# Gated sliding-window attention and channel MLP: early q/k writes, statistics, y and DRAM copies at other steps, first weights in another layout, last output in halves

## The chip, the cores and the metric

The kernel runs on one core of one Trainium2 chip. The metric is the time of one execution on the device in microseconds. A core has five engines with instruction streams of their own: TensorE (PE in the profile, its weight loads are PEld), VectorE (DVE), ScalarE (ACT), GpSimd (POOL) and SyncE (SP), which here only issues DMAs. DMAs are issued by SP and, where named, by ACT; "SPq" and "ACTq" are these issues. Each engine works strictly in the order in which its instructions were written, and waits at an instruction until the semaphores that it needs have come.

## The reference

For x of 2048 tokens by 512 features, two branches are mixed by a gate of each token (cut to what matters):

```python
def _A_ref(x, wqkv, wo):              # H = 32 heads, Dh = 16, W = 256
    q, k, v = split(x @ wqkv)
    scores = einsum("bhqd,bhkd->bhqk", q, k) * (Dh ** -0.5)
    mask = (idx[:, None] - idx[None, :] >= 0) & (idx[:, None] - idx[None, :] < W)
    p = softmax(where(mask, scores, -1e9))
    return merge_heads(p @ v) @ wo
def _B_ref(x, w1, b1, w2, b2):        # F = 1792
    h = gelu(layernorm(x) @ w1 + b1)
    return h @ w2 + b2
g = sigmoid((x * gate_w).sum(-1, keepdims=True))
return g * _A_ref(x, wqkv, wo) + (1 - g) * _B_ref(x, w1, b1, w2, b2)
```

All is float32. To keep its precision, most products are made of three: each operand is split into a high part h in a shorter format and a low part l = x - h, and h*h + h*l + l*h is summed.

## The kernel before, in words

Sizes: tokens go in 4 chunks c of 512 and 16 blocks of 128; features in 4 tiles dt of 128; the heads in 4 groups g of 8, and a group in two halves, which makes 8 attention passes p of 4 heads each; the MLP's 1792 hidden features in 14 tiles f.

**First stage** (from `first_units`, line 242, to `settle`): q, k and v for all tokens, layer-norm statistics, and the normalised x (called y), transposed. Its work is a list of units n = 0 to 47 with three matmul groups of 4 each: `QK(g, t, c)` (line 281) makes q (t = 0) or k (t = 1) of one group and chunk, `vl[b]` (line 305) makes v of a block. Before each unit `tick()` (line 130) advances a step; `after(k, fn)` puts work off by k steps, and `at(n, fn)` (line 542) puts work ahead of unit n. So a step is one unit, and the order of every queue is written by these two.

- `first_units` is the first chunk's q and k, interleaved with the arrival of x and of the first weights. `load_x` loads x chunks on SP and splits them, `copy` (line 121) on ACT and `lo_part` (line 118) on DVE.
- `qk_out` (line 291) evicts q or k from PSUM: ACT copies the high part to a tile t, DVE makes the low part, and both go to DRAM (`qkd`): high, low and, for a second operand order, the high part again. For group 0 the high part is written twice by ACT; for other groups once by ACT, and `double` (line 300) copies it from DRAM to DRAM later. The low part is written by SP a step later.
- `load_stacks` (line 318) loads q and k columns from DRAM into the tile `qk`, the operands of the scores. `gaps` (line 200) fills constant rows.
- `stat_unit` (line 431) takes mean, variance and gate of a block on DVE. `stat_end` (line 444) makes the inverse root on POOL for half the tokens, and puts it into DRAM over a DVE transpose. `load_y` (line 474) loads it back and x with it; its `rest` subtracts and multiplies on POOL (lines 489, 490), and its `fin` splits on ACT and DVE. `load_w1` (line 505) loads and splits MLP weights.
- Every third step from 13 on has an `s_pair` (line 327): scores with tokens as rows, of which DVE takes the row maxima (lines 345, 346). `put_max` (line 350) sends four blocks of maxima over POOL, a DVE transpose and DRAM into extra rows of `qk`; in the second stage its four parts are put off by the numbers of `CHAIN` (line 52), counted in letters of `ORDER`.

All temporaries of this stage are tiles t from 15 buffers in turn (`t2`, line 82): a new one waits until the old one's last reader, a DMA too, is done. PSUM has 4 banks "d" for q, k and v, and 2 for S.

**Second stage** (`run(ORDER)`, line 722): attention passes p = 0 to 7, with the MLP's first product in between. The string `ORDER` gives the order: S is an `s_pair`, T an `st_pair` (line 382: transposed scores, exponential on ACT, masks on POOL), P a `pv` (line 402), f two matmuls of `mlp1_unit` (line 597). S runs ahead of T by ten blocks. At each block kb of a pass, `block` (line 684) issues the stacks for the next pass, and some of the copies of `double`.

**Third stage** (from line 759): gelu and the second MLP product (`mlp2`, line 813, 4 x 14 items), whose results are added to the attention output: `attn_out` (line 768) loads what `pv` stored, scales it and multiplies with wo (line 799). The last item of a chunk adds the sum from PSUM on DVE (line 825) and writes it out by SP (line 826).

A tile "edge" of 128 x 8 float32 values stands at the top end of SBUF, and the large tiles x8 below it.

## Time and profile before

| | us |
|---|---|
| median of 3 runs | 720.76 |
| lowest, highest | 718.58, 721.39 |
| the profiled execution | 721.59 |
| its span on the core | 719.9 |
| first stage, to the first transposed scores | 0 to 154.2 |
| second stage, to the last transposed scores | 154.2 to 504.2 |

The profile is of one execution. Times in it are microseconds from the start of the span unless marked ns. A timeline row has its start, its duration, engine, line, operation, output <- inputs, shapes, the count of merged instructions, and in brackets how long the engine was idle before it and what released it. A row of waits has engine, tile and line, the releaser, and us in total, times, longest. A row of stretches has the busy time and instructions of the five engines, then the granted clock of PE as a share, the mean busy share of the 16 DMA engines, and GB/s. A group's row ends with busy us and mean ns, then idle time before it. A row of the chain has start, duration and what the chain went through. A row of a line's instructions has the count, the durations in ns as lowest/median/highest, and the first and last start.

### The profile page before, as it was taken

How to read it: one execution, taken by the hardware profiler on the slowest of the kernel's cores; microseconds unless marked ns; L12 is line 12 of the kernel's file. 1: busy time of each engine (PE TensorE's matmuls, PEld its weight loads, DVE VectorE, ACT ScalarE, POOL GpSimd, SP SyncE). 2: the span in 40 equal slices, each digit the busy share in tenths (PEclk: the TensorE clock that was granted, in tenths of full speed). 3: DMA queues.
4: the chain of work that ended last, by engine and by line, in shares of the span. 5: the costliest groups of instructions: out<-in, count | busy, mean ns of one | idle time of the engine just before them, and what ended most of it. 6: DMA issues, size and time to landing. Idle time of an engine off the chain costs nothing.

```text
span 719.9 us, 15913 instructions
## 1 busy us (share of the span) xinstructions
PE 702.1 (98%) x5740; PEld 541.8 (75%) x5740; DVE 472.6 (66%) x977; ACT 366.5 (51%) x580; POOL 288.6 (40%) x647
## 2 busy tenths in 40 slices
PE   9899999989999899999999999999999999999997
PEld 6677777767777577777777777777777788888885
DVE  6327886777786577767777687784556745645544
ACT  5323123346778567667777767767533414123121
POOL 9220219975557456555665657558000000000000
PEclk9999999989999999999999999999999999999999
DMA  9999795864667765567746664624865443542531
GB/s 312 287 309 290 217 300 159 279 186 153 204 203 222 227 207 163 169 202 237 214 142 203 188 196 141 187 87 162 264 220 164 159 147 118 164 138 103 180 104 58
DMA packets 102917, 137.92 MB, mean 192 GB/s; under 512 B 13912, under 2 KB 54040, under 8 KB 102712
## 3 DMA queue, kind: packets, MB, share of 16 engines
q1 hardware_dynamic: 95544, 124.59, 55.4%
q10 hardware_dynamic: 7296, 12.32, 5.4%
q8 instruction: 46, 0.75, 0.5%
q14 instruction: 31, 0.25, 0.1%
HBM read 81.53 MB, written 54.30 MB: 189 GB/s over the span
## 4 chain that ended last, share of the span: by engine, by line
PE 68%; DMA 12%; POOL 7%; DVE 4%; SPq 3%; ACT 2%; issue 2%; ACTq 2%; POOLq 0%; DVEq 0%
PE ps_b L609 21%; PE ps_a L820 16%; PE ps_b L410 12%; PE ps_b L391 7%; PE ps_b L336 6%; PE ps_o L799 6%; DMA qk<-t 3%; POOL t L489 3%; POOL t L490 3%; DMA qk<-qk 2%; DMA t<-in_xa 2%; ACTq L297 1%; ACT t L122 1%; DMA t<-in_wqk 1%; DMA wv<-in_wqk 1%
## 5 line engine op out<-in xcount | busy, mean ns | idle before, releaser
L609 PE MATMUL ps_b<-x,w 64*128 64x512 f32 x1344 | 215.1, 399 | 0.7 <-DVE mx L346 0.4
L395 POOL TENSOR_SCALAR_AFFINE_SELECT p<-p 128x256 f32<-128x256 f32 x344 | 131.9, 412 | 97.7 <-ACT p L393 96.9
L393 ACT ACTIVATE p<-ps_b 128x768 f32<-128x768 f32 (+2 forms) x184 | 137.5, 770 | 42.6 <-PE ps_b L391 35.6
L820 PE MATMUL ps_a<-x,t 128*128 128x512 f32 x648 | 154.6, 395 | 0.1
L346 DVE TENSOR_REDUCE mx<-ps_b 128x2 f32<-128x512 f32 x208 | 144.1, 693 | 7.1
L820 PEld LDWEIGHTS ps_a<-x,t 128*128 128x128 f32 x648 | 121.4, 188 | 30.3 <-DVE t L119 0.8
L609 PEld LDWEIGHTS ps_b<-x,w 64*128 64x128 f32 x1344 | 131.7, 188 | 12.6 <-issue 2.8
L345 DVE COPY_PREDICATED ps_b<-tri,ps_b 128x256 f32<-128x256 uint8 x208 | 88.3, 425 | 53.4 <-PE ps_b L336 39.1
L336 PE MATMUL ps_b<-qk 62*128 62x384 f32 (+2 forms) x472 | 86.4, 349 | 6.3 <-DMA qk<-qk 4.0
L391 PE MATMUL ps_b<-qk 50*128 50x384 f32 (+5 forms) x512 | 91.1, 345 | 0.4 <-DVE mx L346 0.3
L287 PE MATMUL ps_d<-x,w 128*128 128x512 f32 x360 | 88.6, 397 | 0.0
L287 PEld LDWEIGHTS ps_d<-x,w 128*128 128x128 f32 x360 | 66.9, 188 | 17.2 <-issue 1.9
L410 PE MATMUL ps_b<-p,v 128*32 128x256 f32 (+1 forms) x1376 | 75.5, 332 | 0.7 <-ACT p L393 0.7
L122 ACT ACTIVATE t<-ps_b 128x512 f32<-128x512 f32 (+1 forms) x112 | 51.9, 490 | 42.2 <-PE ps_b L410 35.5
L395 POOL TENSOR_SCALAR_AFFINE_SELECT x<-x 128x256 f32<-128x256 f32 x136 | 52.4, 411 | 37.9 <-ACT x L393 37.4
L391 PEld LDWEIGHTS ps_b<-qk 50*128 50x128 f32 (+1 forms) x512 | 51.7, 186 | 20.0 <-issue 5.8
L393 ACT ACTIVATE x<-ps_b 128x768 f32<-128x768 f32 (+2 forms) x72 | 55.1, 778 | 18.0 <-PE ps_b L391 13.9
L336 PEld LDWEIGHTS ps_b<-qk 62*128 62x128 f32 (+1 forms) x472 | 47.3, 187 | 22.3 <-issue 7.3
L410 PEld LDWEIGHTS ps_b<-p,v 128*32 128x32 f32 x1376 | 39.1, 110 | 26.7 <-ACT p L393 3.7
L119 DVE TENSOR_TENSOR t<-t,t 128x512 fp32r<-128x512 f32 x70 | 48.5, 692 | 14.6 <-ACT t L122 11.6
L312 PE MATMUL ps_d<-wv,x 128*128 128x512 f32 x192 | 49.5, 406 | 2.9 <-DVE wv L119 2.6
L122 ACT ACTIVATE t<-t 128x512 fp32r<-128x512 f32 x16 | 10.1, 632 | 77.8 <-DVE t L787 39.4
(80 smaller groups left out, 661.7 us busy)
## 6 DMA issues: line engine op xcount, KB each, us to landing
qk<-qk SPq DMA_DIRECT2D x112, 196.0 KB
t<-hp SPq DMA_DIRECT2D x56, 256.0 KB
hp<-t SPq DMA_DIRECT2D x52, 256.0 KB
qk<-t ACTq DMA_DIRECT2D x40, 256.0 KB
qk<-t SPq DMA_DIRECT2D x32, 256.0 KB
osc<-t SPq DMA_DIRECT2D x31, 256.0 KB
t<-in_w SPq DMA_DIRECT2D x28, 256.0 KB
w<-w SPq DMA_DIRECT2D x28, 256.0 KB
```

The costliest lines, as they stand in the source:

```text
L122: act.activation(dst, src, AF.Copy)
L287: pe.matmul(o, a[:, dt * 128:(dt + 1) * 128], b[:, dt * C:(dt + 1) * C], start=n == 0, stop=n == 11)
L312: pe.matmul(o, x[:, a:a + 128], wvs[dt][:, k], start=n == 0, stop=n == 11)
L336: pe.matmul(o[:, e, :n], qs[pr][r:k, qb * 128:qb * 128 + 128], ks[pr][r:k, t0:t0 + n], start=True, stop=True)
L345: dve.copy_predicated(o[:, :, :128], tri, o[:, :, 256:384])
L346: dve.tensor_reduce(m, o[:, :, :256], mybir.AxisListType.X, ALU.max)
L391: pe.matmul(o[:, e, :w], ks[pr][r:k, kb * 128:kb * 128 + 128], qs[pr][r:k, kb * 128:kb * 128 + w], start=True, stop=True)
L393: act.activation(pt[:, :, :w], o[:, :, :w], AF.Exp, scale=0.25)
L395: pool.affine_select(out=pt[:, :, a:a + 128], in_=pt[:, :, a:a + 128], pattern=[[0, 2], [sgn, 128]], base=b, channel_multiplier=-sgn, comp ...
L410: pe.matmul(a[32 * h:32 * h + 32, at:at + w], vs[:, kb, v:v + 32], pts[p, kb][:, h, fr:fr + w], start=n == 0, stop=n == len(parts) - 1, sk ...
L609: pe.matmul(o[:, e], w[kt // 4][r:r + 64, k, m:m + 128], y[r:r + 64, a:a + C], start=n == 0, stop=n == 23)
L820: pe.matmul(accs[c][b], x[:, b * 128:(b + 1) * 128], w, start=f == 0 and n == 0, stop=f == FT - 1 and n == 2)
```

## The change

Nine edits, all of order, place or shape; what is computed stays the same.

- `qk_out`: for group 0 all three writes are issued by SP, two steps later for chunk 0 and one step later for the others; for other groups the high part stays on ACT.
- `load_stacks` of pass 0 at steps 7, 8, 9, 12 in place of 4, 6, 8, 12; the low parts of the v weights at step 4 in place of 5.
- The first weights come in an array of their own, `wq0`, with both t side by side, in pieces of dt 0, dt 1 and dt 2 to 3; `first_units` splits them by dt, and the first x copy goes to DVE.
- Statistics: `stat_end` at 21 and 29 (22 and 30), its write after 2 steps (3); `load_y` at 25 and 33 (26 and 35), with lag 2 (3), and `fin` at lag + 2 (lag + 3); first w1 loads at 38 and 41 (41 and 44).
- `double` copies one t at a time, at every even block of passes 0, 2 and 4; before, both at every odd block from 9 on of passes 0, 1 and 3.
- `CHAIN`'s last number is 30 (28).
- `attn_out(0)` at f = 3 (4), its matmuls after 2 steps (1).
- The last block's last output is computed in halves of 256 columns, and the second half written by ACT.
- "edge" has 104 values per partition (8), 416 bytes in place of 32.

```diff
-CHAIN = (6, 13, 17, 28)
+CHAIN = (6, 13, 17, 30)
...
-    get("edge", "edge", 1, (128, 8))
+    get("edge", "edge", 1, (128, 104))
...
-        def hi(dt):
-            copy(part(h, dt), part(raw, dt))
+        def hi(dt, eng=act):
+            if eng is dve:
+                dve.tensor_copy(part(h, dt), part(raw, dt))
+            else:
+                copy(part(h, dt), part(raw, dt))
...
-        pieces = (slice(0, 128), slice(128, 256), slice(256, 512))
-        for k in pieces:
-            act.dma_start(raws[:, :, k], wqk[0, :, :, k].rearrange("t p n -> p t n"))
+        for a, b in ((0, 1), (1, 2), (2, 4)):
+            act.dma_start(raws[:, a:b], wq0[:, a:b])
...
         for dt in range(DT):
+            k = slice(dt * 128, dt * 128 + 128)
+            if dt == 0:
+                hi(dt, dve)
             for t in range(2):
-                if dt < 3:
-                    k = pieces[dt]
-                    copy(ws[t][:, 0, k], raws[:, t, k])
-                    lo_part(ws[t][:, 1, k], raws[:, t, k], ws[t][:, 0, k])
-                if t == 0:
+                copy(ws[t][:, 0, k], raws[:, dt, t])
+                lo_part(ws[t][:, 1, k], raws[:, dt, t], ws[t][:, 0, k])
+                if dt and not t:
                     hi(dt)
-                    lo(dt)
+            lo(dt)
...
-        for k in (0, 1 + t)[:1 + (g == 0)]:
-            act.dma_start(f32(view(d, [S, DH], [50 * S, HG], [1, C], off=k * DH * S + c * C)), f32(h))
-        after(1, lambda: sp.dma_start(f32(view(d, [S, DH], [50 * S, HG], [1, C], off=(2 - t) * DH * S + c * C)), f32(l)))
+        if g:
+            put(act, 0, h)
+        late = (2, 1, 1, 1)[c] if not g else 1
+        after(late, lambda: [put(sp, k, h) for k in ((0, 1 + t) if not g else ())])
+        after(late, lambda: put(sp, 2 - t, l))
...
-        after(3, lambda: sp.dma_start(view(stat, [32, 4], [128, 32], [1, 32]), s))
+        after(2, lambda: sp.dma_start(view(stat, [32, 4], [128, 32], [1, 32]), s))
...
-            after(lag + 3, fin)
+            after(lag + 2, fin)
...
-            at(3 + 2 * k, rests["v"][dt][k])
+            at(3 + k, rests["v"][dt][k])
...
-        at((4, 6, 8, 12)[c], lambda c=c: load_stacks(0, c * C, C))
+        at((7, 8, 9, 12)[c], lambda c=c: load_stacks(0, c * C, C))
...
-    at(22, lambda: stat_end(0))
-    at(30, lambda: stat_end(1))
+    at(21, lambda: stat_end(0))
+    at(29, lambda: stat_end(1))
...
-    at(26, lambda: load_y(0, 0, KT, 3, pool))
-    at(35, lambda: load_y(1, 0, KT, 3, pool))
-    at(41, lambda: load_w1(0, dve))
-    at(44, lambda: load_w1(1, dve))
+    at(25, lambda: load_y(0, 0, KT, 2, pool))
+    at(33, lambda: load_y(1, 0, KT, 2, pool))
+    at(38, lambda: load_w1(0, dve))
+    at(41, lambda: load_w1(1, dve))
...
-        if p in (0, 1, 3) and kb >= NB // 2 and kb % 2:
-            double((p + 3) // 2, kb // 2 - 4)
+        if p in (0, 2, 4) and kb % 2 == 0:
+            double(p // 2 + 1, kb // 4, 1 - kb // 2 % 2)
...
-                after(1, lambda: mm(h, l))
+                after(1 + (c == 0), lambda: mm(h, l))
...
+            parts = ((0, 512),) if i < NB - 1 or f < FT - 1 else ((0, 256), (256, 512))
+            for m, k in parts:
...
+                    (act if m else sp).dma_start(out[i, :, m:k], u)
...
-        if f == (4 if c == 0 else 2):
+        if f == (3 if c == 0 else 2):
```

More of the change, by code (lines that the diff above doesn't have):

```diff
@@ L295, in qk_out, with put, double @@
         lo_part(l, o, h)
-        for k in (0, 1 + t)[:1 + (g == 0)]:
-            act.dma_start(f32(view(d, [S, DH], [50 * S, HG], [1, C], off=k * DH * S + c * C)), f32(h))
-        after(1, lambda: sp.dma_start(f32(view(d, [S, DH], [50 * S, HG], [1, C], off=(2 - t) * DH * S + c * C)), f32(l)))
-    def double(g, c):
-        for t in range(2):
-            fr, to = (f32(view(qkd[g, t], [S, DH], [50 * S, HG], [1, C], off=k * DH * S + c * C)) for k in (0, 1 + t))
-            sp.dma_start(to, fr)
+        def put(eng, k, s):
+            eng.dma_start(f32(view(d, [S, DH], [50 * S, HG], [1, C], off=k * DH * S + c * C)), f32(s))
+        if g:
[3 more added lines that the diff above has]
+        after(late, lambda: put(sp, 2 - t, l))
+    def double(g, c, t):
+        fr, to = (f32(view(qkd[g, t], [S, DH], [50 * S, HG], [1, C], off=k * DH * S + c * C)) for k in (0, 1 + t))
+        sp.dma_start(to, fr)
     def v_unit(b):
@@ L860, in inp @@
         return nc.dram_tensor(name, list(shape), F32, kind="ExternalInput").ap()
[L862 removed]
+    args = [inp("in_xt", (NCH, 128, DT * C)), inp("in_x2", (2, 128, KT * C)), inp("in_wq0", (128, DT, 2, 128)), inp("in_wqk", (NG - 1, 2, 128, DT * 128)), inp("in_wv", (DT, 128, D)),
             inp("in_wo", (DT, 128, D)), inp("in_xa", (NB, 128, D)), inp("in_gw", (D,)),
@@ L882 @@
     w2 = B_w2.reshape(FT, 128, D)
+    wqk = A_wqkv[:, :2 * D].reshape(DT, 128, 2, NG, HG, DH).transpose(3, 2, 1, 0, 5, 4)
     arrays = {
@@ L885 @@
         "in_x2": f(x2),
-        "in_wqk": f(A_wqkv[:, :2 * D].reshape(DT, 128, 2, NG, HG, DH).transpose(3, 2, 1, 0, 5, 4).reshape(NG, 2, 128, DT * 128)),
+        "in_wq0": f(wqk[0].reshape(2, 128, DT, 128).transpose(1, 2, 0, 3)),
+        "in_wqk": f(wqk[1:].reshape(NG - 1, 2, 128, DT * 128)),
         "in_wv": f(A_wqkv[:, 2 * D:].reshape(DT, 128, D)),
```

23 lines of the change are left out of this document (11 added, 12 removed).

## The prediction

> **What bounds the kernel now.** I read the page first, for the busy shares:
>
> ```profile
> PE 702.1 (98%) x5740; PEld 541.8 (75%) x5740; DVE 472.6 (66%) x977; ACT 366.5 (51%) x580; POOL 288.6 (40%) x647
> ```
>
> PE (TensorE) is the bound almost everywhere, and the change takes no matmul away. So only PE's idle time, 719.9 - 702.1 = 17.8 us, and time at a lower clock can be won. The waits of PE come next (engine, line, releaser: us in total, times, longest), then the stretches at half clock:
>
> ```profile
> PE ps_b L336 <- DMA qk<-qk: 4.0, 2, 3.0
> PE ps_d L312 <- DVE wv L119: 2.6, 1, 2.6
> PE ps_b L336 <- DVE t L119: 1.3, 1, 1.3
> PE ps_b L336 <- ACT v L122: 0.6, 1, 0.6
> PE ps_o L799 <- ACT t L122: 0.6, 1, 0.6
> ...
> 30.90:34.30 3.40, 3.40 (x10) 2.61 (x9) 0.00 (x0) 2.48 (x5) 2.89 (x3) 0.50 0.93 224
> 157.10:163.90 6.80, 5.88 (x28) 4.75 (x30) 5.30 (x11) 3.46 (x7) 1.53 (x4) 0.51 0.65 179
> 249.30:252.70 3.40, 3.40 (x37) 2.17 (x38) 0.98 (x2) 1.20 (x2) 0.77 (x2) 0.51 0.81 224
> ```
>
> In the last three rows the granted clock is the third number from the end. Each half-clock stretch begins within 2.6 us of the end of a wait, and costs half its length: 1.7, 3.4 and 1.7 us. So a wait of 2.6 us costs 4.3, the waits at the end of the first stage (1.3 + 0.6 us) cost 5.3, and one of 3.0 us costs 4.7.
>
> The Trainium skill (TensorE: Matmul & The Clock Gate, "Part 1: The HAM clock gate") has the clock drop after an idle window of about 3.4 us. By that no wait here would cost clock, and the sum below would lose 6.8 us, giving 712.2; the trace halves the clock after 2.6 us and decides.
>
> **The first q and k writes (put on SP), stacks, v weights.** The timeline at the first wait:
>
> ```profile
> 12.58 11.32 PE L287 MATMUL ps_d<-x,w 128*128 128x512 f32 x48
> 22.66 3.67 ACTq L297 DMA_DIRECT2D qk<-t  x2
> 26.39 0.60 ACT L122 ACTIVATE t<-ps_d 128x512 fp32r<-128x512 f32 x1 [3.75 <-DMA qk<-t]
> 27.62 2.49 DVE L119 TENSOR_TENSOR wv<-t,wv 128x512 fp32r<-128x512 f32 x4
> 28.36 6.64 PE L312 MATMUL ps_d<-wv,x 128*128 128x512 f32 x16 [2.59 <-DVE wv L119]
> ```
>
> Two writes hold ACT's sequencer for 3.67 us, so ACT's eviction starts at 26.39. The low part of the v weights stands behind that eviction's DVE half and is late for PE. With all 24 writes of group 0 on SP, ACT has no issue there, and the low part is emitted a step earlier too (step 4, 48 matmuls / 4 = 2.8 us a step). Both remove the wait: **-4.3 us**; the other end is 0, if DVE is still late.
>
> The moved writes come up on SP in front of gaps, stacks and weight loads:
>
> ```profile
> 0.00:20.00 20.00, 18.48 (x68) 12.56 (x69) 12.35 (x24) 11.24 (x22) 17.37 (x19) 1.00 0.92 321
> 20.00:40.00 20.00, 17.10 (x64) 12.76 (x63) 6.07 (x11) 5.66 (x10) 8.59 (x6) 0.91 0.95 281
> ...
> 48.87 0.44 PE L336 MATMUL ps_x<-qk 62*128 62x128 f32 x4
> ...
> L298 SPq DMA_DIRECT2D qk<-t x32: 518/547/1950, 19.5 to 156.1; - x32
> 29.83 7.48 DMA qk<-t
> 12.64 3.72 SPq L224 DMA_DIRECT2D v<-in_xt  x4
> ```
>
> The first consumer is the S matmul of step 13, today at 48.9 us, then at 48.9 - 4.9 = 44.0 (this part and the start below). It needs the first stack, now issued at step 7. Ahead of it lie loads of 5.8 MB, 18 writes of 262 kB, gaps of 0.3 MB and one weight of 0.26 MB; with the stack's 0.8 MB, 11.8 MB. By 40 us today 20 x 321 + 20 x 281 kB = 12.0 MB have moved, at a DMA share of 0.92 to 0.95. So it lands at about 40. SP issues 21 DMAs for it (18 writes, 2 gaps, 1 load); at the median of 0.55 us that is 11.5 us after its last x loads (12.64 + 3.72 = 16.4), and with the slow landing of 7.5 us the end is near 36. Covered by 4 us, so 0; if that cover is gone, the S matmul is late next (rival C). Later stacks have the wider gap of three steps per S.
>
> **The start.** The rows:
>
> ```profile
> 5.35 0.31 ACT L122 ACTIVATE w<-wv 128x128 fp32r<-128x128 f32 x1 [1.72 <-DMA wv<-in_wqk]
> 5.56 0.61 ACT L122 ACTIVATE x<-v 128x512 fp32r<-128x512 f32 x1
> 6.26 6.47 PE L274 MATMUL ps_d<-x,w 128*128 128x512 f32 x24
> ```
>
> The first x copy goes from ACT to DVE, beside the weight's copy, so the first matmul can start near 5.8 instead of 6.26. The 24 matmuls take 6.47 us, against 24 x 11.32 / 48 = 5.66 unbroken. At best 0.45 + 0.8 = 1.2 us; at worst +0.3, one more weight copy of ACT (0.31) in front of the x copies. The same bytes arrive in runs twice as long. I take **-0.6**.
>
> **Statistics, y, first w1.** The end of the first stage:
>
> ```profile
> 103.91 1.29 POOL L489 TENSOR_TENSOR t<-t,t 128x512 f32<-128x512 f32 x1 [16.79 <-DMA t<-in_x]
> L490 POOL TENSOR_TENSOR t<-t,t 128x512 f32<-128x512 f32 x16 | 23.6, 1478 | 1.3
> L489 POOL TENSOR_TENSOR t<-t,t 128x512 f32<-128x512 f32 x16 | 22.9, 1432 | 16.8 <-DMA t<-in_x 16.8
> ...
> 154.77 0.60 ACT L122 ACTIVATE t<-ps_d 128x512 fp32r<-128x512 f32 x1 [4.29 <-POOL t L489]
> 155.40 0.69 DVE L119 TENSOR_TENSOR t<-ps_d,t 128x512 fp32r<-128x512 f32 x1 [3.05 <-ACT t L122]
> 156.15 0.44 PE L336 MATMUL ps_b<-qk 62*128 62x384 f32 x2 [1.31 <-DVE t L119]
> ```
>
> From 103.9 on POOL does 32 such operations (23.6 + 22.9 us), and the second statistics between them. The last q/k eviction takes the buffer that POOL's subtractions read to the end, so ACT waits 4.29 us, DVE 3.05 and PE 1.31. The load of y now comes one step earlier (25, not 26), its statistics two: about 3.0 us, beside the shift of all steps. That is most of ACT's 4.29, and what is left (1.3 us) hides, since ACT's wait of 4.29 reached PE as 1.31. The y operations, the copies and the w1 loads are the same in number.
>
> Against it: the split of y (fin) is now due 3 steps earlier in the first half, while POOL gains one step. ACT and DVE are in order, and what queues behind fin are evictions and the S maxima:
>
> ```profile
> 123.14 0.21 DVE L361 STREAM_TRANSPOSE ms<-nm 128x32 f32<-128x32 f32 x1 [2.99 <-POOL nm L119]
> 128.06 0.69 DVE L346 TENSOR_REDUCE mx<-ps_x 128x2 f32<-128x512 f32 x1
> 131.04 0.62 PE L336 MATMUL ps_x<-qk 62*128 62x384 f32 x4
> ```
>
> DVE's transpose waits for POOL already; the max of an S ends at 128.75, the next S wants its bank at 131.04: 2.3 us of cover. One more pair of POOL operations (1.48 + 1.43 us) will stand before that transpose, so PE may wait 0.6 us, and again after: 1.5 us by my estimate. So -5.3 + 1.5 = **-3.8**; ends 0 and -5.3.
>
> **DRAM copies (double).** Today two at every odd late block of p = 0, 1, 3; then one at every even block of p = 0, 2, 4, behind the stack load of that block.
>
> ```profile
> 241.44 7.10 DMA qk<-qk
> L391 PE MATMUL ps_b<-qk x512: 215/335/522, 154.2 to 504.2; 64*128 64x384 f32 x76, 50*128 50x384 f32 x73, 50*128 50x256 f32 x6, 50*128 50x128 f32 x6
> ```
>
> The eight p share 154.2 to 504.2 us, 44 us each, so the long stack load of 241.44 (7.10 us) lies at the end of p = 1, among that p's copies. PE's list has two waits on stacks, 3.0 and 1.0 us, fewer than the three p with copies; half the copies at a time should do less, and p = 1 and 3 have none left. **-5.7** (3.0 + 1.0 + 1.7 of clock); other end 0, the same waits at p = 2 and 4. CHAIN's last step two places later lets SP wait less:
>
> ```profile
> SPq L370 <- DMA md<-ms: 44.6, 24, 3.5
> ```
>
> PE has no wait on these rows in its list, and the load still follows the landing: 0.
>
> **Attention output and tail.**
>
> ```profile
> 547.78 3.04 PE L799 MATMUL ps_o<-w,t 128*128 128x512 f32 x12 [0.63 <-ACT t L122]
> 549.05 0.57 SPq L784 DMA_DIRECT2D t<-rd  x1
> ...
> 713.52 2.85 DVE L825 SCALAR_TENSOR_TENSOR us<-ps_a,g,us 128x512 f32<-128x512 f32 x4 [2.56 <-PE ps_a L820]
> ```
>
> attn_out(0) starts one step earlier and its matmuls stay at their step: **-0.6**. SP's 32 loads of about 0.57 us then lie before the h loads by one step, 2.8 us, which is the other end (+2.2). In the tail the last DVE operation (2.85 / 4 = 0.71 us) becomes two halves, the first under PE's last matmuls; the last transfer is half as big: **-0.4** (ends 0, if the fixed cost of one more operation and transfer eats it, and -0.8). The tile at the top of SBUF moves right-hand tiles by 384 bytes; matmuls on left and right tiles take 406 and 395 ns in the page's groups:
>
> ```profile
> L820 PE MATMUL ps_a<-x,t 128*128 128x512 f32 x648 | 154.6, 395 | 0.1
> L312 PE MATMUL ps_d<-wv,x 128*128 128x512 f32 x192 | 49.5, 406 | 2.9 <-DVE wv L119 2.6
> ```
>
> so I take 0 (ends 648 x 0.5 ns either way, 0.3 us).
>
> **Sum.** -4.3 - 0.6 - 3.8 - 5.7 - 0.6 - 0.4 = -15.4 us. The profiled execution took 721.59 us (span 719.9 and 1.7 around), so 706.2; the median shown, 720.76, is 0.8 lower: **705.4 us**. All best ends (-4.3 - 1.2 - 5.3 - 5.7 - 0.6 - 0.8 - 0.3 = -18.2) give 702.6.
>
> **Rivals.** *A: the front's gain is held up before 150 us.* The y chain hangs on statistics, whose xa loads share DMAs that are 0.92 to 0.95 busy to 40 us. If only the one step of 3.0 us comes through, the stage ends 3.0 earlier, with a half-clock stretch of 3.4 us left: 3.0 + 3.4 - 1.7 = 4.7 instead of 8.7: 709.4. For it: only 2.3 us of cover; against: POOL's first y operation waited for a load, and that load is moved up. *B: copies collide with stacks again*, at p = 2 or 4: 705.4 + 5.7 = 711.1. For it: the copies are as many; against it: they are spread over twice the blocks. A and B together: 715.1. *D: the releasers are not the cause* and each wait re-forms at the next late thing, S at step 13 and the transposes: 719. Against it: the chain through ACT, DVE and PE above closes without gaps.
>
> *C, slower: SP as the one issuer.* If an issue takes not 0.55 but 2.0 us (its longest was 1.95), the first stack is issued at 16.4 + 21 x 2.0 = 58.4 and lands 8.2 later at 66.6, against 44.0: a wait of 22.6 us and 1.7 of clock, 705.4 + 24.3 = 729.7. It turns to a loss from 1.6 us an issue on. For it: two issues of 3.67 us on ACT; against: the median, and that DMA rate, not issue, held these.
>
> The Trainium skill (DMA: Bandwidth & Descriptors, "Rules for kernel authors") says that spreading DMAs over engines brings no bandwidth and only saves issue time on the sequencers; that is rival C's cost, and no more than its 21 issues.
>
> **How the numbers follow.** Forecast 0.50, A 0.14, B 0.12, both 0.06, D 0.08, C 0.10. Faster than 720.8 by over 0.5% (what a measurement can tell, below 717.2): 0.50 + 0.14 + 0.12 + 0.06 = 0.82; same 0.08; slower 0.10. The forecast's own range is 702.6 to 708; the range, with A, B and both, 701.5 to 716.5.
>
> **What would show it.** Right: PE's list of waits without wv, with under 1.5 us on qk, and no half-clock rows at 31, 157 and 249 us; the last POOL y operation before PE's last v unit ends; L287 to L312 unbroken at 24 us. Wrong: a wait on S at step 13 with SP issuing long (C), waits of PE on L346 before 140 us (A), a wait on a stack at p = 2 or 4 (B).

## The result, and the profile after

The changed kernel took 725.48 us (median of 9 runs, 722.38 to 728.09) beside 720.94 us for the kernel before on the same chip (9 runs, 717.79 to 721.49): a ratio of 1.0081, 95% interval 1.0058 to 1.0103. By the ratio it is slower by about 5.8 us (the medians are 4.5 us apart), where 705.4 us was forecast with a range of 701.5 to 716.5. The profiled execution, 722.38 us with a span of 720.5, is the fastest of the nine, and that of the kernel before, 721.59 us, was slower than all nine of its runs here. So the two traces show 0.6 us of the 5.8: they tell where time goes, and the ratios tell how much.

The busy shares of the changed kernel's page, and its list of PE's waits (engine, tile, line, releaser; us in total, times, longest):

```profile
PE 697.7 (97%) x5743; PEld 543.2 (75%) x5743; DVE 479.3 (67%) x981; ACT 365.3 (51%) x581; POOL 291.2 (40%) x647
```

```profile
PE ps_b L399 <- ACT p L401: 3.7, 1, 3.7
PE ps_a L831 <- DVE t L677: 3.0, 4, 1.8
PE ps_d L290 <- ACT w L122: 2.7, 2, 2.3
PE ps_x L344 <- DVE mx L350: 1.7, 2, 1.5
...
PE ps_a L831 <- DVE us L835: 0.9, 1, 0.9
PE ps_x L344 <- DVE mx L354: 0.9, 2, 0.7
...
PE ps_b L344 <- DMA qk<-qk: 0.8, 2, 0.6
```

The old waits are gone as forecast: none on `wv`, 0.8 us in place of 4.0 on the stacks. But PE's idle time rose from 17.8 to 720.5 - 697.7 = 22.8 us: waits of other names stand in their place. The half clock did not shrink either; it moved (stretches, with the granted clock third from the end):

```profile
51.00:54.40 3.40, 3.40 (x8) 2.75 (x9) 1.47 (x3) 1.29 (x3) 0.00 (x0) 0.50 0.71 229
68.10:71.50 3.40, 3.40 (x9) 2.63 (x9) 3.05 (x10) 0.00 (x0) 0.00 (x0) 0.50 0.85 286
163.60:167.00 3.40, 3.40 (x20) 2.92 (x18) 1.99 (x4) 1.28 (x3) 1.53 (x4) 0.51 0.02 7
532.30:535.70 3.40, 3.40 (x10) 2.63 (x9) 3.33 (x7) 0.00 (x0) 0.00 (x0) 0.50 0.51 164
```

Four stretches of 3.4 us, 13.6 us in all, as before (3.4 + 6.8 + 3.4). And a second surprise lies in the busy time: PE has three instructions more and the same half clock, yet is busy 4.4 us less. So there is a gain that the prediction put at 0, and the losses must be larger than the 5.8 us.

### The profile page after: what moved, and what is told of

Same layout as the page of the kernel before. It is cut to its first block, busy times and chain, and to the rows that moved or that the text cites. A ratio compares the mean times of both kernels' runs of the same rounds, so it can differ in the third digit from the quotient of the medians.

```text
span 720.5 us, 15913 instructions
## 1 busy us (share of the span) xinstructions
PE 697.7 (97%) x5743; PEld 543.2 (75%) x5743; DVE 479.3 (67%) x981; ACT 365.3 (51%) x581; POOL 291.2 (40%) x647
## 4 chain that ended last, share of the span: by engine, by line
PE 71%; DMA 11%; POOL 5%; DVE 4%; SPq 4%; ACT 2%; issue 1%; ACTq 0%; POOLq 0%; DVEq 0%
PE ps_b L617 19%; PE ps_a L831 16%; PE ps_b L418 11%; PE ps_b L399 6%; PE ps_b L344 6%; PE ps_o L807 5%; PE ps_d L290 4%; DMA t<-in_xa 2%; DMA t<-in_wqk 2%; POOL t L498 2%; POOL t L497 2%; DMA qk<-qk 2%; PE ps_d L320 2%; DMA md<-ms 1%; DMA qk<-t 1%
## 5 line engine op out<-in xcount | busy, mean ns | idle before, releaser
L831 PE MATMUL ps_a<-x,t 128*128 128x512 f32 (+1 forms) x651 | 153.9, 393 | 3.9 <-DVE t L677 3.0
L290 PE MATMUL ps_d<-x,w 128*128 128x512 f32 x360 | 90.4, 404 | 2.7 <-ACT w L122 2.7
L290 PEld LDWEIGHTS ps_d<-x,w 128*128 128x128 f32 x360 | 69.0, 194 | 19.8 <-ACT w L122 3.6
L399 PEld LDWEIGHTS ps_b<-qk 64*128 64x128 f32 (+1 forms) x512 | 51.5, 185 | 25.6 <-issue 6.4
L344 PEld LDWEIGHTS ps_b<-qk 62*128 62x128 f32 (+1 forms) x472 | 47.3, 185 | 17.1 <-issue 3.8
L119 DVE TENSOR_TENSOR t<-t,t 128x512 fp32r<-128x512 f32 x70 | 48.5, 692 | 14.5 <-ACT t L122 11.7
L673 ACT ACTIVATE t<-t,b1s 128x512 f32<-128x512 f32 x56 | 38.0, 715 | 26.5 <-DMA t<-hp 25.9
```

The source lines that it names most:

```text
L119: eng.tensor_tensor(out=lo, in0=src, in1=f32(hi), op=ALU.subtract)
L290: pe.matmul(o, a[:, dt * 128:(dt + 1) * 128], b[:, dt * C:(dt + 1) * C], start=n == 0, stop=n == 11)
L344: pe.matmul(o[:, e, :n], qs[pr][r:k, qb * 128:qb * 128 + 128], ks[pr][r:k, t0:t0 + n], start=True, stop=True)
L399: pe.matmul(o[:, e, :w], ks[pr][r:k, kb * 128:kb * 128 + 128], qs[pr][r:k, kb * 128:kb * 128 + w], start=True, stop=True)
L831: pe.matmul(accs[c][b][:, m:k], x[:, b * 128:(b + 1) * 128], w[:, m:k], start=f == 0 and n == 0, stop=f == FT - 1 and n == 2, skip_group_c ...
```

## The experiments

Each ratio is to the kernel before on the same chip, in brackets the 95% interval; 0.001 is 0.72 us. "After" is the changed kernel, 1.0081.

| run | kernel | ratio | median us |
|---|---|---|---|
| e1_edge | before + tile of 416 bytes | 0.9944 [0.9920, 0.9968] | 716.03 |
| e8_edge288 | before + tile of 288 bytes | 0.9987 [0.9959, 1.0015] | 720.54 |
| e9_edge160 | before + tile of 160 bytes | 0.9922 [0.9897, 0.9947] | 715.16 |
| e2_copies | before + `double`'s new steps | 0.9992 [0.9971, 1.0013] | 720.29 |
| e3_attn_back | after without attn_out's edit | 1.0015 [0.9990, 1.0039] | 720.74 |
| e6_halves_back | after without halves | 1.0048 [1.0016, 1.0080] | 725.41 |
| e4_writes_back | after without writes, stacks, v lows | 1.0049 [1.0027, 1.0072] | 722.71 |
| e5_y_back | after without statistics, y, w1 | 0.9985 [0.9961, 1.0008] | 721.09 |
| e10_w1_back | after, w1 at its old steps | 1.0004 [0.9980, 1.0027] | 720.05 |
| e11_late_transpose | after, second transpose later | 1.0062 [1.0039, 1.0085] | 725.33 |
| e7_kept | before + tile, first weights, copies, CHAIN | 0.9933 [0.9902, 0.9963] | 716.30 |
| e12_kept_y | e7 + y, w1 old, transpose later | 1.0012 [0.9992, 1.0032] | 721.05 |
| e13_fin_later | e12 with fin two steps later | 0.9931 [0.9905, 0.9956] | 714.70 |
| e14_shift1 | e7, y chain one step earlier | 0.9956 [0.9936, 0.9977] | 717.38 |
| e15_kept_writes | e7 + writes, stacks, v lows | 0.9939 [0.9916, 0.9963] | 716.14 |
| e16_kept_wvlo | e7 + v lows alone | 0.9946 [0.9928, 0.9965] | 716.40 |
| e17_repaired | e15 + y as in e13 | 0.9895 [0.9862, 0.9927] | 713.46 |
| e18_kept_again | e7 beside e17 | 0.9949 [0.9923, 0.9974] | 717.14 |

### The tile at the top of SBUF

```diff
-    get("edge", "edge", 1, (128, 8))
+    get("edge", "edge", 1, (128, 104))   # e1; e8: (128, 72); e9: (128, 40)
```

> The kernel before with the tile at the top of SBUF at 416 bytes, nothing else. In the changed kernel matmuls that read x8 tiles follow each other at a median of 227 ns, before at 232. Theory (the place of the tiles sets this): 227 ns here too, about 1,200 such matmuls and the first MLP product, 5 to 7 us faster, about 715. Rival (it comes from other edits): 232 ns and 720.9 within 1 us.

Measured 0.9944: 4.0 us faster, from a tile that nothing reads. Where it comes from is in the groups by line, first e1's (busy us, mean ns of one), to be held against the two rows of the kernel before that the prediction showed:

```profile
L820 PE MATMUL ps_a<-x,t 128*128 128x512 f32 x648 | 150.7, 390 | 0.3 <-DVE t L669 0.2
L312 PE MATMUL ps_d<-wv,x 128*128 128x512 f32 x192 | 48.5, 401 | 3.0 <-DVE wv L119 2.7
L799 PE MATMUL ps_o<-w,t 128*128 128x512 f32 x192 | 46.7, 392 | 0.3
```

The 648 matmuls of the second MLP product are busy 150.7 in place of 154.6 us, those of v 48.5 in place of 49.5; those of the attention output are unchanged (46.6 before). From the start of one matmul to the start of the next, within a line, the median of the MLP's fell from 232 to 227 ns; the attention output's is 227 ns in both. The three groups that move (this one, v, and q and k of L287) have 1200 matmuls (648 + 360 + 192), at 5 ns each some 6 us. A part of it may be lost where POOL, which the tile doesn't speed up, ends its y, as e1's list of PE's waits has it (1.3 in the kernel before, one execution each):

```profile
PE ps_b L336 <- DVE t L119: 4.2, 1, 4.2
```

> The kernel before with the edge tile at 72 values, 288 bytes, alone: it moves the tiles below by 256 bytes, where 104 values moved them by 384 and the matmuls stood 227 ns apart in place of 232. If what matters is the place within some larger unit (an address relation of the operands that 384 leaves and 256 doesn't), the spacing stays 232 and the ratio is 1.000. If any shift away from the old place does it: 227 ns, ratio 0.9944. No theory of mine says more than that; the run is to narrow down what the shift changes.

> The kernel before with the edge tile at 40 values, 160 bytes, alone: it moves the tiles below by 128 bytes. A shift of 384 bytes brought the matmuls from 232 to 227 ns apart and the ratio to 0.9944, one of 256 bytes left 232 and 0.9987. Theory (what counts is the place of the two operands to each other within 256 bytes): 128 acts like 384, 227 ns apart, ratio 0.994. Rival (it is the place within 512 bytes or more, or a distance of over 256): the spacing stays at 232 and the ratio is 0.999 to 1.000.

The MLP's group in e8 (a shift of 256 bytes), then in e9 (128 bytes):

```profile
L820 PE MATMUL ps_a<-x,t 128*128 128x512 f32 x648 | 154.4, 395 | 0.1
```

```profile
L820 PE MATMUL ps_a<-x,t 128*128 128x512 f32 x648 | 150.7, 390 | 0.5 <-DVE t L669 0.5
```

Shifts of 0 and 256 bytes give 232 ns, 128 and 384 give 227. By these four shifts what counts is the place within 256 bytes. Which two accesses meet there, the two operands or an operand and another engine's tile, these runs don't tell.

### The DRAM copies

```diff
-        if p in (0, 1, 3) and kb >= NB // 2 and kb % 2:
-            double((p + 3) // 2, kb // 2 - 4)
+        if p in (0, 2, 4) and kb % 2 == 0:
+            double(p // 2 + 1, kb // 4, 1 - kb // 2 % 2)
```

> The kernel before with the DRAM copies at the changed steps alone. Theory (the forecast's term): the waits on stacks, 4.0 us, and one half-clock stretch of 3.4 us go: 5.7 us faster, about 715. Rival: waits of this size come and go from run to run with small delays of the queue, and the median moves by less than 1.5 us.

Measured 0.9992: nothing. The rows on `qk` in e2's list of PE's waits:

```profile
PE ps_b L390 <- DMA qk<-md: 2.5, 3, 1.5
PE ps_b L335 <- DMA qk<-qk: 0.4, 1, 0.4
```

The waits on stacks fell from 4.0 to 0.4 us, as forecast, and 2.5 us came up on the rows of maxima (`md`), which also come over SP's queue and had no wait before. A stretch of half clock stands behind the longest of them, as one stood behind the old wait on the stack. That the copies push this load is borne out by the other traces: all 16 with the copies at the new steps have 1.1 to 3.0 us of PE's waits on `md`, and the four without (before, e1, e8, e9) have none. The waits on stacks don't stay away either: e14, with the new steps, has 3.3 us.

### attn_out and the halves

```diff
-                after(1 + (c == 0), lambda: mm(h, l))
+                after(1, lambda: mm(h, l))
...
-        if f == (3 if c == 0 else 2):
+        if f == (4 if c == 0 else 2):
```

> The changed kernel with the attention output back at f = 4 and one step. Theory (the reciprocal at f = 5 waits on DVE for its load and holds the splits of h behind it): the PE waits on these splits, 1.8 + 0.4 + 0.7 us, and 1.7 us of half clock go, 0.6 us come back: about 4 us faster than the changed kernel, 721.5. Rival (the splits were late anyway): less than 1 us faster.

Measured 1.0015 against 1.0081: the edit costs 4.8 us. The changed kernel's timeline (start, duration, engine, line; in brackets the idle time before and its releaser):

```profile
523.31 2.81 SPq L779 DMA_DIRECT2D su<-osc  x4
...
528.80 0.95 DVE L784 RECIPROCAL su<-su 128x128 f32<-128x128 f32 x1 [6.51 <-DMA su<-osc]
529.67 0.63 DVE L119 TENSOR_TENSOR x<-t,x 128x512 fp32r<-128x512 f32 x1
...
530.21 0.41 DVE L677 CAST t<-t 128x512 fp32r<-128x512 f32 x1
...
530.78 2.84 PE L831 MATMUL ps_a<-x,t 128*128 128x512 f32 x8 [1.78 <-DVE t L677]
```

attn_out begins with a reciprocal on DVE of sums that SP has only just begun to load. DVE, in order, stands 6.51 us at it, and the splits of the h tiles for the next matmuls stand behind. PE pays 1.78 us, then 0.41 and 0.65 behind later splits, and 1.7 us of clock: 4.5 us, which is what the run gives. The same row in e3:

```profile
536.05 0.95 DVE L784 RECIPROCAL su<-su 128x128 f32<-128x128 f32 x1 [4.19 <-DMA su<-osc]
```

One item later, DVE has done more splits ahead, stands 4.19 us, and PE has no wait over 0.3 us from 511 to 717 us.

For the halves, the loop over `parts` and the second DMA queue are taken back:

```diff
-            parts = ((0, 512),) if i < NB - 1 or f < FT - 1 else ((0, 256), (256, 512))
+            parts = ((0, 512),)
```

> The changed kernel with its last output whole again, written by SP alone. Theory: the second half's matmuls wait for DVE's reading of the first half of the same bank (0.89 us in the profile), and the shorter last operation and transfer win back less than that: 0.3 to 0.8 us faster than the changed kernel, ratio 1.007 to 1.008. Prediction: halves gain 0.4, so 0.4 slower here, ratio 1.0087. The times will hardly tell these apart; the profile's last 6 us will: PE's end to the end of the span, and the sum of PE's last 12 or 24 matmuls.

Measured 1.0048, which is 2.4 us better than after, but its interval overlaps that of after, and its median is after's (on another chip, where the kernel before is 0.7 us slower). The trace settles the size. The end of the changed kernel:

```profile
713.67 2.50 DVE L835 SCALAR_TENSOR_TENSOR us<-ps_a,g,us 128x512 f32<-128x512 f32 x4 [2.38 <-PE ps_a L831]
...
716.23 0.62 PE L831 MATMUL ps_a<-x,t 128*128 128x256 f32 x3 [0.89 <-DVE us L835]
716.89 0.48 DVE L835 SCALAR_TENSOR_TENSOR us<-ps_a,g,us 128x256 f32<-128x256 f32 x1 [0.71 <-PE ps_a L831]
```

PE waits 0.89 us for DVE, which reads the first half of the bank whose second half the next matmuls write. From PE's end to the end of the span it is 3.65 us (716.85 to 720.5) where e6 has 4.2 (717.28 to 721.5) and the kernel before 4.3. So the halves win some 0.6 us behind PE and pay 0.9 ahead of it: no gain.

### The first writes, stacks and v weights

```diff
-        if g:
-            put(act, 0, h)
-        late = (2, 1, 1, 1)[c] if not g else 1
...
+        for k in (0, 1 + t)[:1 + (g == 0)]:
+            act.dma_start(...)
...
-            at(3 + k, rests["v"][dt][k])
+            at(3 + 2 * k, rests["v"][dt][k])
...
-        at((7, 8, 9, 12)[c], lambda c=c: load_stacks(0, c * C, C))
+        at((4, 6, 8, 12)[c], lambda c=c: load_stacks(0, c * C, C))
```

> The changed kernel with the first q and k writes, the stacks of pass 0 and the low parts of the v weights at their old steps. Theory (the DMA traffic sets when the later q/k weights land, at 50 and 64 us in both kernels, so PE's early start is waited away): the wait at 26 us comes back, those before 51 and 66 us go, total within 1.5 us of the changed kernel. Rival (the moved writes themselves brought the gain, and something else lost it): 4 us slower.

> The kernel of e7_kept with all 24 first q and k writes on SP, the stacks at 7, 8, 9, 12 and the low parts of the v weights at 4, as in the change. Theory (they bring PE to unit 7 some 5 us earlier, where it waits for q and k weights that land no earlier, and push the S maxima of the first steps together): the wait at 25 (3.59 us and 1.7 of clock) goes, waits of 1.5 to 2.5 us at 48 to 51 and 1 to 2.5 us at 52 to 66 come with 1.7 of clock each: 716 to 719, ratio 0.993 to 0.9975, no gain. Rival (the loss of 2.3 us in the changed kernel came through its y edit): 712 to 713, ratio 0.987 to 0.990.

Taken back from after they win 2.3 us, with intervals that overlap (at most 1.5 were expected); put on e7 they change nothing (0.9939 against 0.9933). The wait at 25 us goes as forecast, and the time is lost again further on. The changed kernel's timeline:

```profile
12.15 11.04 PE L290 MATMUL ps_d<-x,w 128*128 128x512 f32 x48
...
20.98 10.03 SPq L301 DMA_DIRECT2D qk<-t  x12
...
23.03 5.60 PE L320 MATMUL ps_d<-wv,x 128*128 128x512 f32 x24
...
35.43 0.63 ACT L122 ACTIVATE w<-t 128x512 fp32r<-128x512 f32 x1 [3.45 <-DMA t<-in_wqk]
...
50.31 0.63 ACT L122 ACTIVATE w<-t 128x512 fp32r<-128x512 f32 x1 [6.44 <-DMA t<-in_wqk]
...
50.99 1.22 PE L290 MATMUL ps_d<-x,w 128*128 128x512 f32 x2 [2.31 <-ACT w L122]
```

PE runs from q and k into v without a break, and SP issues 12 writes in 10.03 us, 0.84 us each, about half of rival C's 1.6. But of the later q and k weights, loaded behind all this, the first is split at 35.43 and the third only at 50.31. In the kernel before, the third was split at nearly the same time, though the first came later:

```profile
44.12 0.63 ACT L122 ACTIVATE w<-t 128x512 fp32r<-128x512 f32 x1 [5.71 <-DMA t<-in_wqk]
...
50.95 0.63 ACT L122 ACTIVATE w<-t 128x512 fp32r<-128x512 f32 x1 [2.85 <-DMA t<-in_wqk]
```

Its load is issued at 42.26 us in place of 43.74, and the changed kernel's DMAs are 0.97 busy from 20 to 40 us and 0.92 from 40 to 60: PE comes earlier, the weights hardly do. Whether the DMAs' load or the place in SP's order holds them, these runs don't separate. PE waits 2.31 us and 1.7 of clock there, and 1.47 and 1.7 on S maxima at 65 us, 7.2 us where 4.3 were saved. In e15 PE waits 2.5 us at 48 and 1.4 at 54 us, and no half clock follows. Held against e7 matmul by matmul, PE in e15 is 6.0 us ahead at 33 us, 3.2 at 55 and 1.1 at 78; in the changed kernel, held against the kernel before, it goes from 5.2 ahead at 32 to 0.9 behind at 79.

A part of e4's 2.3 us comes from elsewhere: the wait of 3.7 us at the end of the stage, which the next section takes up, is 0.9 and 1.2 us in its trace, with no half clock behind.

```diff
-            at(3 + 2 * k, rests["v"][dt][k])
+            at(3 + k, rests["v"][dt][k])
```

> The kernel of e7_kept with the low parts of the v weights at step 4 in place of 5, alone. Theory (they stand on DVE behind an eviction that waits for ACT, which is held by its own two writes): one step earlier they are ahead of that eviction, the wait of 3.59 us at 25 falls under 1.5, and the q and k weights, which land when they land, take back a part at 45 to 50: 0 to 3 us faster, ratio 0.989 to 0.9933. Rival (the eviction itself is late and the next thing behind it waits as long): 0.9933, with the wait at 25 as before.

With the v weights' step alone (0.9946) the wait at 25 is gone too, so DVE's order was its cause; e16's timeline shows what is late next:

```profile
31.40 2.19 ACT L122 ACTIVATE x<-v 128x512 fp32r<-128x512 f32 x4 [1.43 <-issue]
...
32.08 1.08 PE L290 MATMUL ps_d<-x,w 128*128 128x512 f32 x2 [2.58 <-ACT x L122]
```

ACT splits the next x only after its own writes, and PE waits 2.58 us in place of 3.59.

### Statistics, y and the first w1

The whole edit taken back:

```diff
-        after(2, lambda: sp.dma_start(view(stat, [32, 4], [128, 32], [1, 32]), s))
+        after(3, lambda: sp.dma_start(view(stat, [32, 4], [128, 32], [1, 32]), s))
...
-            after(lag + 2, fin)
+            after(lag + 3, fin)
...
-    at(21, lambda: stat_end(0))
-    at(29, lambda: stat_end(1))
+    at(22, lambda: stat_end(0))
+    at(30, lambda: stat_end(1))
...
-    at(25, lambda: load_y(0, 0, KT, 2, pool))
-    at(33, lambda: load_y(1, 0, KT, 2, pool))
-    at(38, lambda: load_w1(0, dve))
-    at(41, lambda: load_w1(1, dve))
+    at(26, lambda: load_y(0, 0, KT, 3, pool))
+    at(35, lambda: load_y(1, 0, KT, 3, pool))
+    at(41, lambda: load_w1(0, dve))
+    at(44, lambda: load_w1(1, dve))
```

> The changed kernel with the edit of statistics, y and first w1 taken back (stat_end, load_y and its lags, load_w1 at their old steps), all else kept. The changed kernel stands at 1.0081 of the one before, 725.5 us. Theory (the y edit moves a wait instead of removing it): its profile showed PE waiting 3.71 us at 159 (the exponential waits for a tile whose last writes, pushed together by the earlier w1 loads, land at 162) and, in two kernels that share this edit, 4.46 us at 111 to 115 (the maxima of S stand on DVE behind the transpose of the second statistics, late by POOL behind two pairs of y); both are absent here, and what comes back are the old 1.3 and 0.6 us at 155 to 158. So 4 to 8 us faster than the changed kernel: 717.5 to 721.5, ratio 0.996 to 1.002. Rival as predicted (the edit gains 3.8 us): 729, ratio 1.013. Rival nothing in it: 725, ratio 1.008.

0.9985: the edit costs 6.9 us, the largest loss of the change. It has parts. First the w1 loads alone (`at(41)`, `at(44)` for 38 and 41):

> The changed kernel with load_w1 back at steps 41 and 44, the rest of the statistics and y edit kept. The whole of that edit costs 1.0081 - 0.9985, 6.9 us. Theory: two losses. One is the w1 loads, which stand ahead of the last writes of the first stage, so that these land at 162 and the exponential waits for their tile (PE's 3.7 us at 159 and half a clock stretch); it goes here: 3 to 5 us faster than the changed kernel, ratio 1.001 to 1.004, and the wait at 111 to 115 on the S maxima stays. Rival 1 (all of it is the wait at 111 to 115): ratio 1.008, the wait at 159 is there with w1 late as well. Rival 2 (all of it is w1): ratio 0.998.

1.0004: 5.5 us of the 6.9, a little over what was expected. The changed kernel's timeline at the end of the first stage:

```profile
153.91 1.13 SPq L520 DMA_DIRECT2D w<-w  x2
...
155.31 3.91 SPq L301 DMA_DIRECT2D qk<-t  x2
...
161.82 0.81 ACT L401 ACTIVATE p<-ps_b 128x768 f32<-128x768 f32 x1 [4.92 <-DMA qk<-t]
162.68 0.44 PE L399 MATMUL ps_b<-qk 64*128 64x384 f32 x2 [3.71 <-ACT p L401]
```

The half swaps of w1 (`w<-w`) now meet the last writes of q and k. The first exponentials write tiles p that take the memory of the first stage's t; ACT waits 4.92 us until the writes that read it have landed, and PE 3.71. In e10 neither wait is there; PE's longest from 140 to 170 us is 1.4. The 3.71 us and 1.7 of clock (the stretch at 163.6) make 5.4, as measured.

Next the transpose:

```diff
-        after(2, lambda: dve.transpose(s, rt.rearrange("p h a b -> p (h a b)")))
-        after(2, lambda: sp.dma_start(view(stat, [32, 4], [128, 32], [1, 32]), s))
+        after(2 + 2 * half, lambda: dve.transpose(s, rt.rearrange("p h a b -> p (h a b)")))
+        after(2 + 2 * half, lambda: sp.dma_start(view(stat, [32, 4], [128, 32], [1, 32]), s))
```

> The changed kernel with the transpose and write of the second statistics two steps later (4 steps after stat_end, not 2), all else kept. Theory: POOL's arithmetic for it stands behind two pairs of y, ends at about 114 us, and DVE, in order, stands at the transpose with the S maxima behind it; two steps (5.6 us) later the transpose finds its input ready and PE's wait at 111 to 115 (4.5 us and two stretches of half clock, 3.4 us, in most runs) is gone: 3 to 8 us faster than the changed kernel, ratio 0.997 to 1.004, with the wait at 159 still there. Rival (the S maxima are late for another reason, or w1 is all of the loss): 1.007 to 1.008, the wait at 111 to 115 stays.

Its ground was a wait that kernels with the y edit have, here e3's timeline:

```profile
113.58 0.19 POOL L466 COPY rt<-mv 128x8 f32<-128x8 f32 x1
...
113.80 0.21 DVE L468 STREAM_TRANSPOSE ms<-rt 128x32 f32<-128x32 f32 x1 [3.60 <-POOL rt L466]
113.94 0.40 DVE L353 COPY_PREDICATED ps_x<-tri,ps_x 128x256 f32<-128x256 uint8 x1
...
115.21 0.69 PE L344 MATMUL ps_x<-qk 62*128 62x384 f32 x2 [4.46 <-DVE mx L354]
```

After's own trace doesn't have it; e4, e6 and e10 have it with 4.5, 2.8 and 3.4 us. e11 gave 1.0062, 1.4 us better than after and inside the interval, where 3 to 8 us were expected: the wait at 111 to 115 is absent, and waits of 1.92 and 0.67 us on S came up at 121 to 124. The theory named the wait, not the loss. So the rest of the edit was tried on e7, which has none of the other losses:

> The kernel of e7_kept (the kernel before with the tile of 416 bytes, the first weights, the DRAM copies and CHAIN; ratio 0.9933) with the statistics and y edit too, but with the second transpose two steps later and the w1 loads at their old steps. e7_kept lost 3.98 and 0.36 us of waits and 3.4 us of clock at 152 to 161, where the last eviction waits for POOL's y. If the prediction's reason was right and only the transpose and w1 spoiled it, that goes down: 3 to 7 us faster than e7_kept, 710 to 713.5, ratio 0.985 to 0.990. If the y edit is a loss in itself: 716 to 720, ratio 0.993 to 0.999.

1.0012: not 5 us faster than e7, but 5.7 slower, though w1 and the transpose were mended. Held against e7 matmul by matmul, PE in e12 is 0.2 us late at 101 us, 6.3 at 123 and 4.3 to 5.8 from 167 on, so the loss arises between 101 and 123 us. ACT's waits from 100 to 165 us, first in the kernel before and in e7, then in the changed kernel and in e12:

```profile
ACT x L122 <- POOL t L490: 5.4, 5, 3.0
ACT x L122 <- POOL t L492: 14.3, 7, 5.1
```

```profile
ACT x L122 <- POOL t L498: 30.0, 15, 5.3
ACT x L122 <- POOL t L492: 29.0, 15, 6.9
```

With the edit ACT stands at the split of y for POOL's product 15 times, twice as often and as long as in e7, and everything that it should evict stands behind. That is fin, due 4 steps after its load where it was 6. Giving it two steps:

```diff
-            after(lag + 2, fin)
+            after(lag + 4, fin)
```

> The kernel of e12_kept_y (1.0012; it is e7_kept, 0.9933, with the y edit, w1 at its old steps and the second transpose later) with fin put off by lag + 4 steps in place of lag + 2. In e12_kept_y ACT waited 29.0 us in 15 waits for POOL's y (before: 5.4 in 5), with the evictions of v and the S maxima behind it, and PE 1.1 us at 115 and 2.5 us at 122 to 125. Theory (the loss is the split standing in ACT's and DVE's order ahead of its input): those waits go, ACT's sum falls under 12 us, and what is left is POOL's end, one step earlier: 711 to 716, ratio 0.987 to 0.994. Rival (the earlier chain costs through DMAs or tiles, whatever fin does): 0.999 to 1.002.

0.9931, and ACT's row in e13:

```profile
ACT x L122 <- POOL t L492: 10.0, 8, 1.7
```

The 5.8 us are back: fin's place is the loss on e7. (The row is of an execution of 710.46 us, the fastest of ten.) The parts don't add up, though: in after, w1 alone is 5.5 of the 6.9 us, and the rest of the edit, a loss of 5.7 on e7, only 1.4. Against e7 there is no gain in e13. Nor is there from the forecast's plain idea, the whole chain one step earlier with all distances kept:

```diff
-    at(26, lambda: load_y(0, 0, KT, 3, pool))
-    at(35, lambda: load_y(1, 0, KT, 3, pool))
+    at(25, lambda: load_y(0, 0, KT, 3, pool))
+    at(34, lambda: load_y(1, 0, KT, 3, pool))
```

> The kernel of e7_kept (0.9933) with stat_end at 21 and 29 and load_y at 25 and 34, all distances as before (write after 3, lag 3, fin after lag + 3): the whole chain one step, 2.8 us, earlier and nothing else. e7_kept waits 3.98 and 0.36 us at 152 to 161 for POOL's last y, and loses 3.4 us of clock there. Theory (the prediction's reason for a gain: POOL's end sets the last eviction): POOL ends up to 2.8 us earlier, the wait falls to about 1.2, the half clock to one stretch: 3 to 5 us faster, ratio 0.986 to 0.990. Rival (POOL isn't earlier, since its first y waits for its load or since POOL and not the plan sets the pace): within 1.5 us of e7_kept, ratio 0.991 to 0.995.

0.9956. e14's timeline at the end of the stage:

```profile
153.02 1.27 POOL L492 TENSOR_TENSOR t<-t,t 128x512 f32<-128x512 f32 x1
...
154.32 0.60 ACT L122 ACTIVATE t<-ps_d 128x512 fp32r<-128x512 f32 x1 [4.57 <-POOL t L492]
...
157.21 0.69 PE L338 MATMUL ps_b<-qk 62*128 62x384 f32 x2 [4.07 <-ACT v L122]
```

POOL's last y operation starts at 153.02 where e7's starts at 155.27, 2.25 us sooner. PE waits 4.07 as in e7 (3.98): the eviction of q or k is released sooner, but the last v stands on ACT behind splits of y and w1.

### What is left

> The kernel before with four edits only: the tile of 416 bytes, the first weights' layout with the first copy on DVE, the DRAM copies at every even block, CHAIN 30. No edit of writes, stacks, v weights, statistics, y, attn_out or halves. Theory: the tile gives 4.0 us, the first weights 0.5, the copies and CHAIN nothing: 716.2, ratio 0.9935, and the waits of 2.6 us on the v weights and of 1.3 and 0.6 us at the end of the first stage are there as before. Rival (the other edits are losses only beside some of these four, so that CHAIN or the first weights carry a part of the loss): 718 to 722, ratio 0.997 to 1.002.

0.9933, as expected: the tile's gain, and no loss. Its waits on the v weights and at the end of the first stage were not as expected, though: 3.6 and 4.0 us, not 2.6 and 1.3. Then the change once more with the losses out of it: e15's kernel with e12's y edit and e13's fin.

> The changed kernel without its attn_out and halves edits, with w1 at its old steps, the second transpose two steps later and fin after lag + 4. Theory (the steps of the prediction hold once their side losses are gone): waits at 25 and at 152 both absent, beside new ones at 49 and 55: 708 to 713, ratio 0.983 to 0.990. Rival (each gain in the first stage is taken back by the next late thing, weights at 49 or POOL, DVE and ACT at 110 to 165, as in e14 to e16): 714 to 717, ratio 0.991 to 0.9955.

> The kernel of e7_kept once more, beside e17 on one chip: 0.9933 again, 715 to 717; its waits at 25 (3.6 us) and 152 (4.0 us) as in e7.

Side by side on one chip e17 gave 0.9895, by the ratio just inside what its theory gave, and e18 0.9949, 3.7 us apart in the medians; the intervals just touch. e18 has its waits as expected (3.8 and 4.0 us). It and e7 are one kernel, and their profiled executions took 719.31 and 716.37 us, with 17.1 and 10.2 us of half clock while PE works: so much does one trace differ from the next. e17's rows of PE's waits:

```profile
PE ps_x L344 <- DVE mx L354: 3.2, 2, 2.8
PE ps_d L290 <- ACT w L122: 2.8, 1, 2.8
```

The waits at 25 and at 152 to 161 us are both gone, and two of 2.8 us stand at 48 and 129. Half clock stands behind each, 6.8 us twice. The version is the fastest measured, 7.2 us below the kernel before in the medians, and more than half of that is the tile's (4.0 in e1). That the first stage's edits earn some 3.7 us when both are in and repaired, and nothing one at a time, is what these numbers suggest; the touching intervals don't prove it.

## Why the prediction was wrong

The step that failed is the sum: it takes each wait that goes as time won, 15.4 us in all, and prices what the edits themselves hold up at 1.5 us. Taken one at a time none of these gains is measured clear of the noise, and four of the edits cost 10.7 us together. Only the tile, put at 0, hides part of it; without its 4.0 us the change would lose some 10, if the terms add up. A slower kernel had a chance of 0.10, all of it for rival C, which isn't what happened.

| term | forecast us | measured us |
|---|---|---|
| first writes, stacks, v lows | -4.3 | +2.3 in after (e4), +0.4 on e7 (e15) |
| statistics, y, w1 | -3.8 | +6.9 (e5) |
| DRAM copies | -5.7 | -0.6 (e2) |
| attn_out | -0.6 | +4.8 (e3) |
| halves | -0.4 | about +0.3 by the trace; +2.4, uncertain, by e6 |
| start | -0.6 | -0.4 in the trace (the row of L287 starts at 12.58, of L290 at 12.15) |
| tile | 0 | -4.0 (e1) |

A difference of two ratios is uncertain by some 2 us, and the terms aren't independent: taken back one at a time the four losses are 16.4 us, all together (e7 against after) 10.7. CHAIN and the first weights were run only within e7.

**Right** was the reading of what two of the waits hung on: the v weights behind DVE's order (e16), the stacks beside the copies (e2, though not in every trace). For the last eviction behind POOL's y it holds by half: with POOL 2.25 us sooner PE waits as long for the next thing (e14), and with the whole edit the wait is gone (e13, e17). Rival C fell as argued.

**The start: near by luck.** The first matmul was to start near 5.8 us instead of 6.26; it starts at 6.51. The gain is that the 24 matmuls then take 5.80 us in place of 6.47, and a little of that is the tile's.

**The first writes: the gain was followed to the first consumer only.** The prediction checked that the S of step 13 wouldn't be late, and stopped. The next operands due from a saturated DMA, the q and k weights, were not looked at, though ACT's waits of 5.71 and 2.85 us for them stood in the trace of before. Rival D said it ("each wait re-forms at the next late thing") and had 0.08; that half of it is what happened here, though its 719 had no losses in it.

**Statistics and y: the wait that the edit adds was mis-sized.** The prediction saw that fin is due three steps earlier while POOL gains one, and that DVE and ACT are in order, and then priced it at 1.5 us by one transpose with 2.3 us of cover. The runs show 15 waits of ACT with 29.0 us (e7: 7 with 14.3), worth 5.8 us (e12 to e13). It also said that the w1 loads "are the same in number" and gave their place no price: 5.5 us (e10). The cover that was lost there is the landing of the last writes, on which the next stage's tiles wait.

**Copies: the sum took for granted that a wait removed is time won.** The load of the maxima was costed at 0 because PE had no wait on it; it had none only while the copies stood at their old steps. That is rival B, at p = 2, with the other load as its victim.

**attn_out: the wrong neighbour.** The range's bad end, +2.2, was SP's issue time. What stands in the way is DVE's reciprocal: it waits for its load, and the splits are behind it.

**The tile: a mean was read as a bound.** 0 came from two group means, 406 against 395 ns, taken for a left and a right tile. Both groups read tiles that move, each fell by 5 ns in e1, and their difference says nothing of the place. The spacing of starts, in the trace of before 232 ns in these groups against 227 in the attention output, would have shown 5 ns on 1200 matmuls.

On the clock, the rule of a half-clock stretch behind each wait holds for nearly all waits over 2 us (not for 2.5 us at 48 us in e15), and below that only sometimes; the last section shows on what it hangs. The case for the Trainium skill's idle window (TensorE: Matmul & The Clock Gate, "Part 1: The HAM clock gate"), about 3.4 us, is no better than it was: in the changed kernel the clock halves behind 2.31 us.

## What to carry to other kernels

Where, as here in the first 60 us, every engine runs in order and the DMAs are over 0.9 busy, a wait that is removed is worth only the distance to the next thing that is due: list the next two or three operands of PE with the time at which each is ready, before adding up the waits. An instruction that is brought forward without its input blocks all that is behind it on its engine, so the distance between producer and consumer should move with it, not shrink. Compare the spacing of like matmuls on different tiles: where it differs, moving a tile by 128 bytes may be worth more than a reordering, as it was here. And hold two traces against each other matmul by matmul: the place where the distance changes is where the time is lost.

## What the runs showed of the hardware

- The spacing of matmuls depends on where their tiles stand within 256 bytes, as far as four shifts show: 232 ns at shifts of 0 and 256 bytes, 227 ns at 128 and 384, 2% less for the matmuls concerned and 4.0 (e1) to 5.6 us (e9) of the kernel. The cause isn't known.
- The half clock comes in pieces of 3.41 us (3.4, 6.8, in e18 10.2), and not by the length of a wait alone: behind waits of 1.47 and 1.78 us the clock halved in the changed kernel, behind 1.25 and 1.79 us in e13 it did not.
- What decides, for the most part, is where a wait falls. Within each of the 20 traces all stretches start whole multiples of 3.41 us apart (in the changed kernel at 51.00, 68.07, 163.64 and 532.28: 5, 28 and 108 pieces), so one grid runs through an execution. Take the pieces of that grid at full clock, without the first 20 and the last 12 us: all 40 in which PE stood idle for 1.89 us or more were followed by half clock, 13 of the 35 with 1.20 to 1.83 us, and none with less. A wait that a grid line cuts in two can therefore go free, as 1.79 us in e13 (1.44 in the longer part) and 2.5 us in e15 (1.68).
